# An attention and gated-MLP kernel on one core: the opening written in another order, with fillers on TensorE, the first rest values pooled by GpSimd, and the last weight loaded in halves

## The chip, the cores and the metric

The kernel runs on one core of a Trainium2 chip. The metric is the time of one execution in microseconds on the device. Three runs of the kernel before are shown, with their median, and one further execution was profiled.

The engines are named as the profile names them: PE (TensorE, matrix products), PEld (its weight loads), DVE (VectorE), ACT (ScalarE), POOL (GpSimd) and SP, whose queue issues nearly all transfers.

## The reference

```python
def _attn_ref(q, k, v):                       # q, k, v: 8 x 8 x 576 x 64
    k_p = k.reshape(B, H, S // 8, 8, D).mean(axis=3)
    v_p = v.reshape(B, H, S // 8, 8, D).mean(axis=3)
    scores = np.matmul(q, k_p.transpose(0, 1, 3, 2)) / np.sqrt(D)
    scores = scores - np.max(scores, axis=-1, keepdims=True)
    attn = np.exp(scores)
    attn = attn / (np.sum(attn, axis=-1, keepdims=True) + 1e-09)
    return np.matmul(attn, v_p).astype(np.float32)

def _moe_ref(x, w_in, w_out):                 # 4608 x 512, 512 x 2048, 2048 x 512
    h = x @ w_in
    g = h * np.clip(h + 3.0, 0.0, 6.0) / 6.0
    return (g @ w_out).astype(np.float32)
```

Keys and values are means over 8 positions, so each of the 8 batches has 72 keys. The attention's output, 8 batches of 576 tokens by 512, is the x of the second function. The two weights come as 64-bit floats.

## The kernel before

**Precision.** The large products take fp32r operands, each value split into a high and a low part; a product is three matmuls (high by high, high by low, low by high). x, g and the weights are split this way. Batch 0's scores, transposes and attention products use plain float32.

**Blocks and steps.** The 4608 tokens are cut into blocks of 512, 256 and then ten of 384 (L22). The weights stay on the chip, in 16 slices f of 128 hidden columns. A step (`Step`, L584) is one slice for one block: `h` (12 matmuls into a bank of PSUM), `relu` on ACT, `gate` on DVE, `hi` on ACT, `lo` on DVE, and `out` (three matmuls for each tile of 128 tokens, added up over the slices). `run` (L788) goes through a block's steps; `out` follows two steps behind `h`. Between the matmuls `slot` places the attention of the next block, piece by piece.

**The first block** carries more. Its 512 tokens belong to batch 0 and are two parts, A (tokens 0 to 255) and B (256 to 511). Their attention is done in the opening, L676 to L766. Its steps also prepare the weights, since each slice arrives as 64-bit words. For one slice `Prep` (L480) does `scale` and `low` on ACT, `sign` and `join` on DVE, then `hi` on ACT and `lo` on DVE, each over 1024 columns (w_in's half and w_out's half together). Slice 0 alone is loaded and prepared in two halves of 512 columns. During the block's later steps batch 1's keys and values are loaded and pooled.

**What sets the order.** A planner orders the instructions of each engine by its own timeline, within the dependencies. Inside `in_order()` (L89) the instructions of PE, DVE and ACT keep the order in which they are written: each gets a dependency on the one before it on its engine. POOL and SP are left to the planner there too. The whole opening is written out this way; so are `relu` to `lo` and the weight preparation of the first block's steps (L798), and the pooling of batch 1's keys and values (L144, L252). Each engine takes its instructions one after another, so an instruction that waits holds up all behind it.

**The opening, in order.** `busy(13)` writes 13 products of the identity into a bank that nobody reads, while the first transfers run. Then `prep_k` pools the keys (DVE) and ACT scales them into `kbd`. A has four score tiles (two tiles of tokens, two groups of heads): `product` on PE, `top` on DVE (the negated maximum), `exps` on ACT (four exponents with their sums), `invert` on DVE, `divide` on POOL or DVE. `FirstValues` pools batch 0's values on PE: `heads` adds eight slices by products with the identity, `place_heads` copies them on ACT; `rest` does the same for the 8 keys of each head that don't fit 64 rows, and `place_rest` masks them on DVE into `vrem`. `transposes` turns the attention on PE and copies it out (DVE or ACT). `av` is the attention product, two float32 matmuls for each of four columns of heads, with the second one reading `vrem`; `put_x` splits the result into `xhi` (ACT) and `xlo` (DVE). Slice 0's step for A follows, a[0], with B's scores, transposes and `av` around it. The second half of slice 0, for B, is the first step of `run`; its `h` isn't in written order, so the planner sets its matmuls between others.

**Memory.** The first loads lie in regions ("stage") that later hold weights 7 to 14. The region of slice 15 holds the work tile `u` of the preparation, two halves for even and odd slices. So slice 15 can be loaded only when slice 14 is done with `u`. In `run`, step 13 (k = 15) loads it whole, and prepares it in two parts: `scale` to `join` in the same step, `hi` and `lo` in the next.

## Time and profile before

| | us |
|---|---|
| median of three runs | 963.69 |
| lowest, highest | 961.54, 964.84 |
| the profiled execution | 961.42 |
| its span, first to last instruction | 959.6 |

The mean granted clock of the profiled execution is 0.993 of full speed. Where the busy shares of PE are below nine tenths in the page's 40 slices (24 us each), the slices are the first three and the last:

```profile
PE   8799989999999999999999999999999999999998
PEld 6577768899999999999999999999999998999996
DVE  5788975747424437436433444634633442442221
ACT  4578755645334426435435345434534453532322
POOL 1000340403001103102201010300300110110000
PEclk9899999999999999999999999999999999999999
```

A row is one engine and a digit the tenths of a slice in which it was busy; in the last row a digit is the granted clock in tenths. Times below are microseconds from the first instruction. A line such as "L555" is a line of the kernel before. In rows of grouped instructions stand the count, then busy time and the mean in nanoseconds, then the idle time ahead of them and what ended it.

### The profile page before, as it was taken

The numbers are of one execution on the slowest core, as the hardware profiler recorded it, in microseconds if no ns is written. First come the engines' busy times: TensorE is split into PE (matmuls) and PEld (weight loads), VectorE is DVE, ScalarE is ACT, GpSimd is POOL, SyncE is SP. The second block draws the span as 40 slices with busy tenths as digits, with TensorE's granted clock in tenths as the row PEclk, the third lists the DMA queues.
The fourth block names the chain that finished last, engine by engine and source line by source line (L and its number), as shares of the span: only waits on it lengthen the run. The fifth ranks groups of instructions, "written<-read, shape, count | busy, mean of one in ns | idle before, by whom it ended". The sixth has DMA issues, their size and how long they took to land.

```text
span 959.6 us, 13759 instructions
## 1 busy us (share of the span) xinstructions
PE 936.5 (98%) x4934; PEld 832.6 (87%) x4934; DVE 467.4 (49%) x986; ACT 448.0 (47%) x1388; POOL 130.4 (14%) x247
## 2 busy tenths in 40 slices
PE   8799989999999999999999999999999999999998
PEld 6577768899999999999999999999999998999996
DVE  5788975747424437436433444634633442442221
ACT  4578755645334426435435345434534453532322
POOL 1000340403001103102201010300300110110000
PEclk9899999999999999999999999999999999999999
DMA  9942013313001104004001004102201000100000
GB/s 338 397 158 67 17 45 105 95 36 107 12 26 31 35 1 153 24 1 153 12 1 55 12 24 129 48 1 93 72 1 37 19 23 1 45 1 1 33 1 33
DMA packets 42452, 58.57 MB, mean 61 GB/s; under 512 B 3600, under 2 KB 24080, under 8 KB 42384
## 3 DMA queue, kind: packets, MB, share of 16 engines
q1 hardware_dynamic: 42240, 57.69, 18.0%
q8 instruction: 39, 0.64, 0.3%
q14 instruction: 29, 0.24, 0.1%
q10 hardware_dynamic: 144, 0.00, 0.0%
HBM read 48.24 MB, written 9.44 MB: 60 GB/s over the span
## 4 chain that ended last, share of the span: by engine, by line
PE 82%; DVE 4%; ACT 3%; DMA 1%; issue 1%; SPq 0%; ACTq 0%; POOL 0%; DVEq 0%
PE pso L626 37%; PE psh L597 37%; PE psa L415 3%; PE psa L295 3%; PE psa L368 2%; DVE w L555 1%; ACT e L303 1%; DVE u L516 1%; ACT raw L522 1%; DMA vst<-v_l 1%; DVE vst L253 1%; DVE g L609 1%; ACT u L511 0%; DMA raw<-w_out_l 0%; DVE u L527 0%
## 5 line engine op out<-in xcount | busy, mean ns | idle before, releaser
L597 PE MATMUL psh<-xhi,w 128*128 128x384 f32 (+2 forms) x1544 | 432.3, 340 | 7.5 <-DVE w L555 5.0
L626 PE MATMUL pso<-w,ghi 128*128 128x512 f32 x1152 | 360.6, 402 | 2.1 <-ACT ghi L613 2.1
L597 PEld LDWEIGHTS psh<-xhi,w 128*128 128x128 f32 x1544 | 281.0, 189 | 23.9 <-DVE w L555 7.8
L597 PE MATMUL psh<-xlo,w 128*128 128x384 f32 (+2 forms) x772 | 260.0, 337 | 0.0
L626 PEld LDWEIGHTS pso<-w,ghi 128*128 128x128 f32 x1152 | 207.2, 188 | 33.7 <-ACT ghi L613 2.3
L605 ACT ACTIVATE g<-psh,small 128x384 f32<-128x384 f32 (+2 forms) x193 | 112.5, 583 | 240.3 <-PE psh L597 240.0
L626 PE MATMUL pso<-w,glo 128*128 128x512 f32 x576 | 219.6, 396 | 1.2 <-DVE glo L617 1.2
L609 DVE SCALAR_TENSOR_TENSOR g<-g,psh 128x384 f32<-128x384 f32 (+2 forms) x193 | 106.1, 550 | 225.4 <-ACT g L605 224.5
L597 PEld LDWEIGHTS psh<-xlo,w 128*128 128x128 f32 x772 | 146.0, 189 | 9.9
L613 ACT CAST ghi<-g 128x384 fp32r<-128x384 f32 (+2 forms) x193 | 99.5, 516 | 74.2 <-DVE g L609 71.8
L617 DVE TENSOR_TENSOR glo<-g,ghi 128x384 fp32r<-128x384 f32 (+2 forms) x193 | 108.9, 565 | 51.6 <-ACT ghi L613 49.4
L329 POOL TENSOR_TENSOR a<-e,sm 128x256 f32<-128x256 f32 x72 | 47.7, 663 | 634.6 <-DVE sm L320 407.7
L626 PEld LDWEIGHTS pso<-w,glo 128*128 128x128 f32 x576 | 107.7, 188 | 27.8 <-DVE glo L617 2.8
L303 ACT ACTIVATE e<-psa,mx 128x72 f32<-128x72 f32 x288 | 89.2, 330 | 52.6 <-DVE mx L299 50.3
L299 DVE TENSOR_REDUCE mx<-psa 128x4 f32<-128x288 f32 x80 | 35.2, 453 | 56.0 <-PE psa L295 55.8
L303 ACT ACTIVATION_READ_ACCUMULATOR e<-psa,mx 128x1 f32 x288 | 61.6, 214 | 0.0
L409 DVE TENSOR_TENSOR xlo<-psa,xhi 128x192 fp32r<-128x192 f32 (+3 forms) x68 | 29.6, 438 | 37.8 <-ACT xhi L408 37.7
L253 DVE TENSOR_REDUCE vst<-vst 128x64 f32<-128x512 f32 (+1 forms) x42 | 44.8, 1072 | 6.1 <-DMA vst<-v_l 3.4
L408 ACT CAST xhi<-psa 128x192 fp32r<-128x192 f32 (+3 forms) x68 | 25.9, 384 | 45.2 <-PE psa L415 44.4
L295 PE MATMUL psa<-kbd,qt 128*128 128x144 f32 x280 | 43.4, 286 | 0.4 <-ACT kbd L153 0.4
L295 PEld LDWEIGHTS psa<-kbd,qt 128*128 128x128 f32 x280 | 40.6, 189 | 2.1 <-ACT kbd L153 0.6
L379 DVE TENSOR_TENSOR alo<-psa,ahi 128x256 fp32r<-128x256 f32 (+1 forms) x70 | 27.7, 396 | 24.4 <-ACT arem L378 24.3
(67 smaller groups left out, 620.1 us busy)
## 6 DMA issues: line engine op xcount, KB each, us to landing
qt<-q_l SPq DMA_DIRECT2D x36, 256.0 KB, 3.5
out<-o SPq DMA_DIRECT2D x36, 256.0 KB, 2.1
raw<-w_in_l SPq DMA_DIRECT2D x16, 512.0 KB, 10.1
raw<-w_out_l SPq DMA_DIRECT2D x16, 512.0 KB, 10.1
kst<-k_l SPq DMA_DIRECT2D x28, 288.0 KB, 3.7
vst<-v_l SPq DMA_DIRECT2D x28, 256.0 KB, 3.9
vst<-vr_l SPq DMA_DIRECT2D x42, 64.0 KB, 1.9
stage<-k_l SPq DMA_DIRECT2D x4, 288.0 KB, 3.4
```

Of the source, the lines that this page charges most:

```text
L253: nc.vector.tensor_reduce(out=vs, in_=st[:n, : POOL * D].rearrange("p (o d) -> p d o", o=POOL), axis=AX.X, op=ALU.add)
L295: nc.tensor.matmul(to, qt[:, p, :], kbd[:, p, :], start=True, stop=True)
L299: nc.vector.tensor_reduce(out=self.mx, in_=self.ps, axis=AX.X, op=ALU.max, negate=True)
L303: nc.scalar.activation(self.e[:, h], self.ps[:, h], AF.Exp, bias=self.mx[:, h : h + 1], accum_out=self.sm[:, h : h + 1])
L329: engine.tensor_tensor(out=self.a[:, : 4 * D].rearrange("p (h s) -> p h s", h=4), in0=e[:, :, :D], in1=sm[:, :, None].broadcast_to([P, 4, D]),
L409: nc.vector.tensor_tensor(out=xlo, in0=ps, in1=xhi.bitcast(F32), op=ALU.subtract)
L597: nc.tensor.matmul(self.ps, l[f][:, c, :], r[:, c, :], start=c == 0 and i == 0, stop=c == NCC - 1 and i == 2)
L605: nc.scalar.activation(self.g, self.ps, AF.Relu, bias=half, scale=1.0 / (6.0 * WSCALE))
L609: nc.vector.scalar_tensor_tensor(out=g, in0=g, scalar=1.0, in1=self.ps, op0=ALU.min, op1=ALU.mult)
L613: nc.scalar.copy(self.ghi, self.g)
L617: nc.vector.tensor_tensor(out=self.glo, in0=self.g, in1=self.ghi.bitcast(F32), op=ALU.subtract)
L626: nc.tensor.matmul(pos, l, r[f], start=f == 0 and i == 0, stop=f == NF - 1 and i == 2)
```

## The change

The change has four parts.

1. **The opening in another order.** After A's score products six fillers are written, five more ahead of B's first `av`, and two ahead of its last two. B's first score product moves ahead of A's `av`, the second and third between and behind them, over more banks. Slice 0's preparation starts earlier (its first `scale` and `low`, and the second `scale`, ahead of `place_heads`; `sign` and `join` ahead of A's transposes), and its second half is finished later, between B's softmaxes. B's softmaxes all use `exps`, the form with sums on ACT. All of B's `av` moves ahead of the second half of slice 0, whose `h` is now in written order (in `run`, for steps of part of a block). Slice 1 is fully prepared at the end of the opening, `hi` and `lo` too, and `run` skips what is prepared (the set `prepared`). For B's last two `av` the low part of x is written down behind slice 1's `hi`.
2. **The rest's values on POOL.** `rest` adds the eight slices in three halving steps in place and masks them, all on POOL; `place_rest` and the products on PE are gone.
3. **Batch 1's pooling** of keys and values is no longer in the written order.
4. **The last slice** is loaded in two tiles, one for each half of `u`. Both transfers are written one step earlier (k = 14); the first half needs only slice 13 to be done with `u`, the second slice 14. The first half is prepared wholly in step 13, the second half in steps 13 and 14.

```diff
@@ -141,10 +141,9 @@
         if i == 0:
             ksum[b, g] = pool.tile([P, 2, SP], F32, name="ksum", bufs=1)
         ks = ksum[b, g]
-        with in_order() if b == 1 else nullcontext():
-            nc.vector.tensor_reduce(
-                out=ks[:, i], in_=kraw.pop((b, p)).rearrange("p (s o) -> p s o", o=POOL), axis=AX.X, op=ALU.add
-            )
+        nc.vector.tensor_reduce(
+            out=ks[:, i], in_=kraw.pop((b, p)).rearrange("p (s o) -> p s o", o=POOL), axis=AX.X, op=ALU.add
+        )
         if i == 1:
 
             scale = 1.0 / (POOL * D**0.5)
@@ -227,14 +226,14 @@
                 nc.scalar.mul(self.v32[rows, :, h * D : (h + 1) * D], self.ps[rows], 1.0 / POOL)
 
         def rest(self):
-            self.pr = att_bank()[:REM, : NG * D].rearrange("p (g d) -> p g d", g=NG)
-            self.add(self.pr, vraw[0, NPAIR])
-
-        def place_rest(self):
+
+            raw = vraw[0, NPAIR]
+            for w in (4 * D, 2 * D, D):
+                nc.gpsimd.tensor_tensor(out=raw[:, :, :w], in0=raw[:, :, :w], in1=raw[:, :, w : 2 * w], op=ALU.add)
             for g in range(NG):
-                nc.vector.tensor_tensor(
+                nc.gpsimd.tensor_tensor(
                     out=self.vrem[:, g].rearrange("p (h d) -> p h d", h=4),
-                    in0=self.pr[:, g, None, :].broadcast_to([REM, 4, D]),
+                    in0=raw[:, g, None, :D].broadcast_to([REM, 4, D]),
                     in1=mask[:REM, 2:6, None].broadcast_to([REM, 4, D]),
                     op=ALU.mult,
                 )
@@ -249,10 +248,9 @@
         n, h = (P, 2) if p < NPAIR else (3 * REM, 4)
         st = vraw.pop((b, p))
         vs = st[:n, POOL * D : (POOL + 1) * D]
-        with in_order() if b == 1 else nullcontext():
-            nc.vector.tensor_reduce(
-                out=vs, in_=st[:n, : POOL * D].rearrange("p (o d) -> p d o", o=POOL), axis=AX.X, op=ALU.add
-            )
+        nc.vector.tensor_reduce(
+            out=vs, in_=st[:n, : POOL * D].rearrange("p (o d) -> p d o", o=POOL), axis=AX.X, op=ALU.add
+        )
         m = mask[:n, :2] if p < NPAIR else mask[:n, 2:6]
         raw = st[:n, : h * D]
         nc.gpsimd.tensor_tensor(
@@ -403,17 +401,16 @@
             mms = [(whi[:, p], hi[:, i, :T]), (whi[:, p], lo[:, i, :T]), (wlo[:, p], hi[:, i, :T])]
         return mms + [(wrem[:, g, i * P : (i + 1) * P], rem[:, :T])]
 
-    def put_x(j, T, x0, p, ps):
-        xhi, xlo = (t[:, p, x0 : x0 + T] for t in x_block(j))
-        nc.scalar.copy(xhi, ps)
-        nc.vector.tensor_tensor(out=xlo, in0=ps, in1=xhi.bitcast(F32), op=ALU.subtract)
-
-    def av(j, b, h0, T, x0, p):
+    def av(j, b, h0, T, x0, p, later=None):
+
         ps = att_bank()[:, :T]
         mms = av_sums(b, h0, T, p)
         for n, (l, r) in enumerate(mms):
             nc.tensor.matmul(ps, l, r, start=n == 0, stop=n == len(mms) - 1)
-        put_x(j, T, x0, p, ps)
+        xhi, xlo = (t[:, p, x0 : x0 + T] for t in x_block(j))
+        nc.scalar.copy(xhi, ps)
+        low = lambda: nc.vector.tensor_tensor(out=xlo, in0=ps, in1=xhi.bitcast(F32), op=ALU.subtract)
+        low() if later is None else later.append(low)
 
     def side_steps(b):
 
@@ -463,13 +460,14 @@
 
 
     def groups(f):
-        return [(0, 1), (1, 2)] if f < SPLIT else [(0, 2)]
+        return [(0, 1), (1, 2)] if f < SPLIT or f == NF - 1 else [(0, 2)]
 
     def w_tile(name, f, a, b, shape, dtype):
-        return const.tile([P, b - a] + shape, dtype, name=f"{name}_{f}", tag=f"w_{f}_{a}" if f < SPLIT else f"w_{f}")
+        tag = f"w_{f}" if (a, b) == (0, 2) else f"w_{f}_{a}"
+        return const.tile([P, b - a] + shape, dtype, name=f"{name}_{f}", tag=tag)
 
     def load_w(f):
-        wraw[f] = []
+        wraw.setdefault(f, [])
         for a, b in groups(f):
             raw = w_tile("raw", f, a, b, [DM, 2], U32)
             wraw[f].append((a, b, raw))
@@ -489,15 +487,13 @@
 
 
         def __init__(self, f):
-            self.f, self.raws, self.made = f, wraw.pop(f), {}
-            if f == 0:
-                ubuf.append(const.tile([P, 2, 2 * DM], F32, name="u", tag=f"w_{NF - 1}"))
-            if f == NF - 1:
-                _, _, raw = self.raws[0]
-                self.parts = [(i, i + 1, raw[:, i : i + 1], ring("u")[:, :DM]) for i in range(2)]
-            else:
-                u = ubuf[0][:, f % 2]
-                self.parts = [(a, b, raw, u[:, a * DM : b * DM]) for a, b, raw in self.raws]
+            self.f, self.made = f, {}
+            if f < 2:
+                ubuf.append(const.tile([P, 2 * DM], F32, name="u", tag=f"w_{NF - 1}_{1 - f}"))
+            last = f == NF - 1
+            self.parts = [
+                (a, b, raw, ring("u")[:, :DM] if last else ubuf[f % 2][:, a * DM : b * DM]) for a, b, raw in wraw.pop(f)
+            ]
 
         def words(self, part):
             _, _, raw, u = part
@@ -558,13 +554,17 @@
 
     preps = {}
 
+    prepared = set()
+
     def prep(f, *stages, part=None):
+
         if f not in preps:
             preps[f] = Prep(f)
-        parts = preps[f].parts
         for s in stages:
-            for x in parts if part is None else parts[part : part + 1]:
-                getattr(preps[f], s)(x)
+            for n, x in enumerate(preps[f].parts):
+                if part in (None, n) and (f, s, n) not in prepared:
+                    prepared.add((f, s, n))
+                    getattr(preps[f], s)(x)
 
 
     n_h = [0]
@@ -673,6 +673,7 @@
     values = FirstValues()
     first = Block(0, ["o0", "o1", "o2", "o3"])
     a = [Step(first, f, 0, 2) for f in range(SPLIT)]
+    by_act = nc.scalar.copy
     with in_order():
         busy(13)
         for p in range(NPAIR):
@@ -680,6 +681,7 @@
         x00, x10, x01, x11 = (Scores(*t[:2], g) for g in range(NG) for t in tiles(A))
         for x in (x00, x10, x01, x11):
             x.product()
+        busy(6)
         x00.top()
         x00.exps()
         x10.top()
@@ -702,68 +704,75 @@
         x11.invert()
         x11.divide(nc.vector)
         values.rest()
+        prep(0, "scale", "low", part=0)
+        prep(0, "scale", part=1)
         values.place_heads()
+        prep(0, "sign", "join", part=0)
         T0, T1 = tiles(A)
         transposes(*T0, 0, 0)
         transposes(*T1, 0, 0)
-        values.place_rest()
-        prep(0, "scale", "low", part=0)
-        transposes(*T0, 1, 0, nc.scalar.copy)
-        transposes(*T1, 1, 0, nc.scalar.copy)
-        prep(0, "sign", "join", "hi", "lo", part=0)
+        transposes(*T0, 1, 0, by_act)
+        transposes(*T1, 1, 0, by_act)
+        prep(0, "hi", "lo", part=0)
+        turn = [(t, g) for g in range(NG) for t in tiles(B)]
+        b = [Scores(*t[:2], g) for t, g in turn]
+        att_banks[:] = ["h0", "o0", "o1", "o2", "a0", "a1"]
+        b[0].product()
         av(0, *A, 0)
-        prep(0, "scale", part=1)
+        b[0].top()
+        b[1].product()
         av(0, *A, 1)
-        prep(0, "low", part=1)
+        b[0].exps()
+        b[1].top()
         av(0, *A, 2)
         av(0, *A, 3)
-        prep(0, "sign", "join", "hi", part=1)
-        att_banks[:] = ["a0", "a1", "o2", "o3"]
-        turn = [(t, g) for g in range(NG) for t in tiles(B)]
-        b = [Scores(*t[:2], g) for t, g in turn]
-        b[0].product()
-        b[1].product()
-        a[0].h()
+        att_banks[:] = ["o0", "o2"]
         b[2].product()
-        b[3].product()
-        b[0].top()
-        b[0].exps()
-        prep(0, "lo", part=1)
-        b[1].top()
-        b[1].shift()
-        a[0].relu()
-        a[0].gate()
-        b[1].exp()
-        a[0].hi()
         b[0].invert()
         b[0].divide(nc.gpsimd)
-        a[0].lo()
-        b[1].total()
+        b[1].exps()
+        a[0].h()
+        b[2].top()
+        b[3].product()
         b[1].invert()
         b[1].divide(nc.vector)
-        b[2].top()
+        prep(0, "low", part=1)
+        a[0].relu()
         b[2].exps()
+        a[0].gate()
         b[3].top()
-        b[3].shift()
-        b[3].exp()
+        att_banks[:] = ["a0", "a1", "h0"]
+        transposes(*turn[0][0], turn[0][1], 256)
+        transposes(*turn[1][0], turn[1][1], 256, by_act)
+        prep(0, "sign", "join", part=1)
+        a[0].hi()
+        b[2].invert()
+        b[2].divide(nc.gpsimd)
+        prep(0, "hi", part=1)
+        a[0].lo()
+        b[3].exps()
+        prep(0, "lo", part=1)
+        busy(5)
+        av(0, *B, 0)
+        av(0, *B, 1)
+        prep(1, "scale", "low")
+        b[3].invert()
+        b[3].divide(nc.vector)
         a[0].out()
         att_banks[:] = ["a0", "a1"]
-        transposes(*turn[0][0], turn[0][1], 256)
-        transposes(*turn[1][0], turn[1][1], 256, nc.scalar.copy)
-        b[2].invert()
-        b[2].divide(nc.gpsimd)
-        b[3].total()
-        b[3].invert()
-        b[3].divide(nc.vector)
-        prep(1, "scale", "low", "sign")
-        av(0, *B, 0)
-        av(0, *B, 1)
         transposes(*turn[2][0], turn[2][1], 256)
-        transposes(*turn[3][0], turn[3][1], 256, nc.scalar.copy)
-        prep(1, "join")
-        av(0, *B, 2)
-        av(0, *B, 3)
-        prep(2, "scale", "low", "sign")
+        transposes(*turn[3][0], turn[3][1], 256, by_act)
+        prep(1, "sign", "join")
+        prep(2, "scale")
+        later = []
+        busy(2)
+        av(0, *B, 2, later)
+        av(0, *B, 3, later)
+        prep(1, "hi")
+        for low in later:
+            low()
+        prep(1, "lo")
+        prep(2, "low", "sign")
     for f in range(4, NF - 1):
         load_w(f)
 
@@ -794,24 +803,30 @@
             slot = paced.slot if u >= first_slot else no_slot
             if u < len(steps):
                 x, k = steps[u], preps.get(u)
-                x.h(slot)
+                with in_order() if x.n < x.blk.nt * P else nullcontext():
+                    x.h(slot)
                 with in_order() if x.blk.j == 0 else nullcontext():
                     if k:
                         prep(k - 1, "hi", "lo")
+                    if k == NF - 1:
+                        prep(k, "scale", "low", part=0)
                     x.relu()
                     x.gate()
-                    if k and k < NF - 1:
+                    if k == NF - 1:
+                        prep(k, "sign", "join", part=0)
+                    elif k:
                         prep(k, "join")
                     x.hi()
                     x.lo()
                     if k and k + 1 < NF - 1:
                         prep(k + 1, "scale", "low", "sign")
-                    if k == NF - 1:
-                        load_w(k)
-                    if preps and u == len(steps) - 3:
-                        prep(NF - 1, "scale", "low", "sign", "join")
+                    if k == NF - 2:
+                        load_w(NF - 1)
+                    elif k == NF - 1:
+                        prep(k, "hi", "lo", part=0)
+                        prep(k, "scale", "low", "sign", "join", part=1)
                     elif preps and u == len(steps) - 2:
-                        prep(NF - 1, "hi", "lo")
+                        prep(NF - 1, "hi", "lo", part=1)
             if u == len(steps) - 1:
                 paced.upto(len(attention))
             if u >= lag:
```

## The prediction

> **What bounds the kernel now.** I read the page first, then the waits of PE, then the windows.
>
> ```profile
> span 959.6 us, 13759 instructions
> PE 936.5 (98%) x4934; PEld 832.6 (87%) x4934; DVE 467.4 (49%) x986; ACT 448.0 (47%) x1388; POOL 130.4 (14%) x247
> PE pso L626 <- ACT ghi L613: 2.1, 1, 2.1
> PE psa L415 <- ACT a L373: 2.1, 1, 2.1
> ```
>
> PE is busy for 98% of the span, so only 23 us of idle time exist. Its longest waits in the opening (each row: us in total, times, longest) are 2.1 us for the gated values and 2.1 us for the transposed attention. A second loss is not idle time: the granted clock. In the windows the columns are the stretch, its length, PE, PEld, DVE, ACT and POOL busy, then the clock.
>
> ```profile
> 28.20:31.60 3.40, 2.10 (x10) 1.38 (x11) 3.05 (x11) 1.04 (x3) 0.99 (x2) 1.00 1.03 411
> 31.60:35.00 3.40, 1.29 (x8) 0.68 (x7) 2.78 (x10) 3.01 (x13) 0.81 (x2) 1.00 1.03 411
> 35.00:38.40 3.40, 3.40 (x7) 1.45 (x8) 2.03 (x4) 1.78 (x4) 0.00 (x0) 0.50 1.03 405
> 45.20:48.60 3.40, 1.48 (x8) 0.82 (x7) 2.89 (x4) 3.40 (x11) 0.00 (x0) 1.00 1.09 367
> 48.60:52.00 3.40, 3.06 (x7) 2.51 (x8) 2.44 (x8) 3.40 (x15) 1.21 (x3) 0.51 1.04 410
> 55.40:134.00 78.60, 72.67 (x322) 57.45 (x321) 69.71 (x95) 58.28 (x113) 19.50 (x20) 0.98 0.12 36
> 130.50:133.90 3.40, 2.82 (x7) 2.27 (x8) 2.86 (x4) 1.97 (x3) 3.32 (x2) 0.51 0.01 2
> 134.00:154.00 20.00, 19.54 (x102) 16.22 (x100) 10.90 (x22) 10.38 (x33) 2.51 (x5) 1.00 0.20 66
> ```
>
> A stretch in which PE was busy for 1.29 or 1.48 of 3.4 us is followed by one at half clock; after 2.10 the clock stayed. From 55.4 to 134 PE lacks 5.9 us and DVE is busy for 69.7 of 78.6: here two engines are near their limit. From 134 to 154 only 0.5 us is missing. So three stages can gain: the opening, the first block's middle, and hardly the last weight.
>
> The Trainium skill, "TensorE: Matmul & The Clock Gate" (HAM oscillation), warns of PE gaps above about 3.4 us. By that rule gaps of 2.1 us would not have slowed anything and fillers would be worth nothing; the rows above disagree, and the measurement decides.
>
> **The opening.** I write the new order out as a timetable: each engine takes its instructions in the written order, an instruction starts when its engine and its inputs are ready, I allow 0.06 us from engine to engine, and durations are those of before at full clock.
>
> ```profile
> 2.38 5.70 PE L203 MATMUL idle<-ident 128*128 128x128 f32 x26 [2.38 <-POOL ident masks.py:199]
> 7.92 2.13 PE L295 MATMUL psa<-kbd,stage 128*128 128x144 f32 x16
> 11.67 5.55 PE L218 MATMUL psa<-stage,ident 128*128 128x256 f32 x32 [1.62 <-DMA stage<-v_l]
> 15.29 1.66 PEld L218 LDWEIGHTS psa<-stage,ident 32*32 32x32 f32 x16 [0.33 <-issue]
> 17.15 1.53 PE L368 MATMUL psa<-ident,stage 128*128 128x128 f32 x12
> 18.64 0.67 PE L415 MATMUL psa<-a,v 128*128 128x256 f32 x2
> 23.62 1.25 PE L295 MATMUL psa<-kbd,stage 128*128 128x144 f32 x8
> 26.07 1.14 PE L295 MATMUL psa<-kbd,stage 128*128 128x144 f32 x8
> 45.17 0.28 PE L597 MATMUL psh<-xhi,w 128*128 128x256 f32 x1
> 15.46 0.77 ACT L227 ACTIVATE v<-psa 64x256 f32<-64x256 f32 x2 [3.16 <-PE psa L218]
> 17.74 0.76 DVE L373 COPY a<-psa 128x256 f32<-128x256 f32 x2 [3.05 <-PE psa L368]
> raw<-w_in_l SPq DMA_DIRECT2D x1, 512.0 KB, 5.8
> raw<-w_out_l SPq DMA_DIRECT2D x1, 512.0 KB, 6.3
> ```
>
> PE's terms: a filler is 5.70/13 = 0.44 us. Six of them run from 10.05 (7.92 + 2.13) to 12.6; the values land at 11.67, so they cost 0.9 us there. The sums of heads take 15.29 - 11.67 = 3.6; the small sums of the rest (15.29 to 17.15, 1.9 us) leave PE. Four transposes take 18.64 - 17.15 = 1.5, a score product 2.13/4 = 0.53, four 'av' 23.62 - 18.64 = 5.0. The 'h' of 256 tokens began after two score products at 23.62 + 1.06 = 24.7 and ended at 26.07, 1.4 us; 'out' of two tiles has half its matmuls, each of twice the columns, so I put it at 1.4 too (an estimate). The new order then reads:
>
> 10.05 + 2.6 fillers + 3.6 heads + 1.5 transposes + 2.1 products of B + 5.0 av + 1.4 h + 1.5 transposes of B + 2.2 for five fillers + 5.0 av of B + 1.4 out + 0.9 for two fillers + 1.4 h of the second half = 38.7 us, if PE never waits. Before, that 'h' ended at 45.17 + 0.28 = 45.5.
>
> Does PE wait? ACT's 'scale' and 'low' of weight 0 now stand ahead of place_heads. The halves were issued at 7.22 and 8.10 and land 5.8 and 6.3 us later, at 13.0 and 14.4; three operations of about 0.65 are done by 15.1, and the heads are summed at 16.2. Their cover is ACT's idle 3.16 us; a landing over 1.1 us later would push place_heads back by the excess. 'sign' and 'join' (0.69 each) lie in DVE's idle 3.05 us; without it they would delay the first attention copies by 1.4. What queues behind an input not yet there: the transposes' copies, then av. Followed through all three queues, av of B starts at 29.0 with its last copy ready at 28.4, 'out' at 31.5 with its last input at 30.3, and one wait remains, 0.4 us for the copies of B's last transposes. So 39.1.
>
> From there ACT and DVE set the time, by preparing weights.
>
> ```profile
> L303 ACT ACTIVATE stage<-psa,mx 128x72 f32<-128x72 f32 x16 | 4.9, 322 | 3.8 <-DVE mx L299 3.8
> L522 ACT ACTIVATE raw<-raw 128x1024 f32<-128x1024 f32 x4 | 4.6, 1159 | 0.0
> 52.60 1.23 DVE L516 SCALAR_TENSOR_TENSOR u<-raw,u 128x1024 uint32<-128x1024 uint32 x1 [1.55 <-ACT u L511]
> 53.74 1.22 DVE L555 TENSOR_TENSOR w<-u,w 128x1024 fp32r<-128x1024 f32 x1
> ```
>
> Four exponents take 4.9/4 = 1.2 us, an ACT pass over a weight 1.1, and a DVE pass starts 53.74 - 52.60 = 1.14 after the one before. ACT's queue after A's last x copy (24.1): exponents 25.3, half a 'low', relu and exponents 27.6, copies of B's first transposes 28.4, ghi and half a 'hi' 29.6, exponents 30.8, two x copies of B 31.9, 'scale' and 'low' of weight 1 34.0. DVE's 'sign' and 'join' of it end at 36.4; ACT copies the rest of B's x by 37.9, 'hi' ends at 38.9, DVE's 'lo' at 40.1. Weight 2 on DVE: 'sign' and 'join' 2.3, the half step's gate and glo 0.8, 1.1 of waiting for ACT's 'low' of weight 3, that weight's 'sign' and then 'lo' 2.3: 46.6. Before, weight 2's 'lo' ended at 53.74 + 1.22 = 55.0. **Opening: 46.6 - 55.0 = -8.4 us.** From there both orders have the same work ahead, so the whole rest shifts.
>
> The bounds: PE's idle pieces between 39 and 46.7 come to 3 us, at most 1.55 of them in one stretch of 3.4: a busy 1.85, between the 1.48 that slowed the clock and the 2.10 that did not. A stretch at half clock costs up to 1.7. And if the six fillers buy nothing, their 0.9 is the loss.
>
> **The rest's values on POOL**: per pair three additions and two products on 32 partitions, which the trace does not show. The nearest rows:
>
> ```profile
> 13.84 0.24 POOL L335 TENSOR_TENSOR stage<-stage,sm 128x32 f32<-128x32 f32 x1
> L272 POOL TENSOR_TENSOR vrem<-vst,vrem 32x256 fp32r<-32x256 f32 x2 | 3.1, 1562 | 0.1
> L272 POOL TENSOR_TENSOR vrem<-vst,vrem x14: 727/742/2380, 131.6 to 685.2; 32x256 fp32r<-32x256 f32 x14
> ```
>
> The additions have 512, 256 and 128 elements a partition. By the median 0.74 for 256: 1.5 + 0.74 + 0.4 + 2 x 0.74 = 4.1 us; by the 1.56 of the two in the first block, 8.6. POOL is free at 14.1 (13.84 + 0.24), so they end at 18.2 or 22.7; the first av's second product wants them at 18.8. I take 4.1, since the median is that of 14 and the 1.56 of a crowded DVE: no delay; the other end costs 3.9. Ended ahead of x01's 'divide' instead, they would delay that by about as much as it has to spare.
>
> The Trainium skill, "SBUF — State Buffer" (Who interferes with whom), speaks against this move: a DVE instruction with two SBUF inputs and a POOL instruction that reads SBUF exclude one another. DVE's 'sign' and 'join' stand just there. The two L272 rows bear the rule out in kind; by it the 3.9 would be more likely.
>
> **The first block's middle.** Pooling batch 1's keys and values leaves the written order; the planner places it.
>
> ```profile
> L253 DVE TENSOR_REDUCE vst<-vst 128x64 f32<-128x512 f32 x4 | 4.3, 1065 | 0.0
> L516 DVE SCALAR_TENSOR_TENSOR u<-raw,u 128x1024 uint32<-128x1024 uint32 x11 | 14.1, 1279 | 7.0 <-ACT u L511 6.9
> 126.49 2.92 DVE L253 TENSOR_REDUCE vst<-vst 128x64 f32<-128x512 f32 x3
> 131.08 1.22 PE L597 MATMUL psh<-xhi,w 128*128 128x512 f32 x2 [3.19 <-DVE w L555]
> ```
>
> Three pinned reductions at 126.49 stand ahead of the 'lo' that PE awaits for 3.19 us until 131.08. DVE idles 6.9 us behind 'low' in this stage; reductions that slide in there no longer delay 'lo'. At best PE's 5.9 us and the 1.7 of half clock return, 7.6; but then DVE would be busy for 69.7 of 71. At worst the planner puts each of six value reductions (about 1.07, of which a slot hides little) just ahead of a 'lo': +5, six times some 0.85. I take -2.5, most of the 3.19 stall.
>
> **The last weight.** Its first half's transfer leaves a step earlier; with 0.5 us missing from 134 to 154 I count 0, ends -0.5 and +1 (ACT in line behind the second half's transfer; PE's queue of 'out' covers more than that).
>
> **Sum.** The profiled execution took 961.42 (span 959.6): 961.4 - 8.4 - 2.5 = 950.5. The median of the runs, 963.69, lies 2.3 above it, the mean of all four 1.5; I add that and say 952.
>
> **The rivals.**
> 1. POOL's values come late: for it, DVE's two-input operations beside them; against it, 0.6 us to spare. +1 to +3.9, about 955.
> 2. The freed reductions give part back. For: DVE has little room. Against: the stall that they make now is the longest of the stage. +5 in place of -2.5: about 959.5.
> 3. Slower: the planner puts the value reductions ahead of their transfers, and DVE stands, the weights' preparation behind it.
>
> ```profile
> vst<-v_l SPq DMA_DIRECT2D x4, 256.0 KB, 2.7
> vst<-vr_l SPq DMA_DIRECT2D x6, 64.0 KB, 1.9
> DMA vst<-v_l: 3.4, 9
> ```
>
> Price: four of 2.7 and two of 1.9, 14.6, and the -2.5 is lost: 952 + 17.1 = 969. It decides from 11 us on, three quarters of those transfers. Against it: DVE's unpinned value reductions of later batches waited for such transfers 3.4 us in nine cases altogether.
> 4. The change does nothing, its fillers only taking the place of waits while ACT's queue is as late as before: 963 to 964. The 39.1 for 45.5 speaks against it.
>
> **How the numbers follow.** Forecast 0.64 (947 to 955), rival 1 0.13, rival 2 0.13, rival 3 0.07, rival 4 0.03. A measurement of this kernel tells about 0.3%, 2.9 us, from no change; rival 2 lies at that bound, half of it on either side. Faster 0.64 + 0.13 + 0.06 = 0.83, same 0.07 + 0.03 = 0.10, slower 0.07. The range runs from 946.5, the middle's best end with a little kept back, to 959, which takes in the forecast, rival 1 and some of rival 2.
>
> **What would show it.** Right: weight 2's 'lo' ends near 46.6; no PE wait above 1 us between 12 and 38, and no half clock there; POOL's last operation on the rest ends by 18.8; no PE wait above 2 us in the rest of the block. Wrong: an opening that gains under 5 us breaks the timetable; PE waiting for vrem is rival 1; DVE waiting for vst is rival 3.

## The result and the profile after

The kernel after takes 947.01 us (median of four runs, 946.30 to 947.97), the kernel before 962.65 in the same comparison (961.54 to 964.84, four runs): a ratio of 0.9835, interval 0.9812 to 0.9859. The profiled execution fell from 961.42 to 947.71, its span from 959.6 to 945.9.

The page of the kernel after, and its waits of PE in the first 200 us (us in total, times, longest):

```profile
span 945.9 us, 13775 instructions
PE 931.2 (98%) x4944; PEld 831.6 (88%) x4944; DVE 465.5 (49%) x980; ACT 449.3 (47%) x1402; POOL 130.6 (14%) x252
PEclk9998999999999999999999999999999999999999
```

```profile
PE psa L366 <- POOL vlo L265: 3.1, 1, 3.1
...
PE psa L409 <- DVE a L371: 1.3, 1, 1.3
```

The two waits of 2.1 are gone. In the clock row the low slice is the fourth, where it was the second. A new wait of 3.1 has come. Its windows of the same stretches (columns as before):

```profile
31.60:35.00 3.40, 3.38 (x18) 2.29 (x17) 2.42 (x9) 3.40 (x11) 0.31 (x1) 1.00 1.03 408
...
45.20:48.60 3.40, 2.80 (x17) 1.86 (x15) 2.92 (x5) 2.44 (x6) 0.44 (x2) 1.00 1.10 371
55.40:134.00 78.60, 75.46 (x345) 62.15 (x344) 71.51 (x104) 61.33 (x132) 17.32 (x24) 0.96 0.17 52
73.60:77.03 3.43, 1.03 (x7) 0.72 (x5) 3.43 (x6) 0.68 (x5) 3.43 (x4) 1.00 0.22 59
77.03:80.45 3.42, 2.68 (x8) 2.31 (x9) 3.13 (x7) 2.60 (x10) 3.17 (x6) 0.50 0.41 107
80.45:83.86 3.41, 3.41 (x9) 2.64 (x9) 3.41 (x5) 3.24 (x7) 2.03 (x3) 0.50 0.14 33
134.00:154.00 20.00, 20.00 (x117) 17.47 (x116) 8.94 (x20) 10.12 (x32) 0.69 (x2) 1.00 0.38 124
```

In the opening TensorE is now nearly full and at full clock. At 73.6 it stands, and the clock is halved for the next 6.8 us.

To see where the time went, I note when TensorE reaches the same amount of work in both kernels. Work is the sum of the usual start-to-start spacing of the products, without fillers and without the rest's small sums (a reckoning from the rows of both traces, us):

```
work done    before    after   difference
    8         19.86    20.16      +0.3     A's scores and heads
   56         80.63    72.60      -8.0     opening
   60         85.16    81.86      -3.3     the new stop and its half clock
  100        133.81   123.08     -10.7     before's stop at 127.9, half clock
  104        137.85   127.04     -10.8     end of the middle
  152        189.81   175.66     -14.2     last weight, rest of the block
  500        540.08   525.98     -14.1     nothing more
```

So 8.0 come from the opening, 2.8 from the middle and 3.3 from the last weight. After the first block nothing changes.

### The profile page after: what moved, and what is told of

Its sections match the earlier page's. It is cut to its first block, busy times and chain, and to the rows that moved or that the text cites. A ratio compares the mean times of both kernels' runs of the same rounds, so it can differ in the third digit from the quotient of the medians.

```text
span 945.9 us, 13775 instructions
## 1 busy us (share of the span) xinstructions
PE 931.2 (98%) x4944; PEld 831.6 (88%) x4944; DVE 465.5 (49%) x980; ACT 449.3 (47%) x1402; POOL 130.6 (14%) x252
## 4 chain that ended last, share of the span: by engine, by line
PE 93%; DVE 3%; ACT 2%; issue 1%; DMA 1%; POOL 0%; SPq 0%; ACTq 0%; POOLq 0%
PE pso L626 41%; PE psh L597 41%; PE psa L409 4%; PE psa L293 4%; PE psa L366 2%; DMA stage<-q_l 1%; DVE u L512 0%; DVE u L523 0%; DVE w L551 0%; DVE mx L297 0%; ACT u L507 0%; DVE vst L251 0%; DVE ksum L144 0%; ACT w L546 0%; ACT e L301 0%
## 5 line engine op out<-in xcount | busy, mean ns | idle before, releaser
L327 POOL TENSOR_TENSOR a<-e,sm 128x256 f32<-128x256 f32 x72 | 47.9, 665 | 616.8 <-DVE sm L318 401.1
L317 DVE TENSOR_SCALAR sm<-sm 128x4 f32<-128x4 f32 x80 | 15.2, 190 | 50.7 <-ACT e L301 50.4
## 6 DMA issues: line engine op xcount, KB each, us to landing
raw<-w_in_l SPq DMA_DIRECT2D x16, 512.0 KB, 10.1
raw<-w_out_l SPq DMA_DIRECT2D x16, 512.0 KB, 10.1
```

The lines of the kernel that those rows point to most:

```text
L327: engine.tensor_tensor(out=self.a[:, : 4 * D].rearrange("p (h s) -> p h s", h=4), in0=e[:, :, :D], in1=sm[:, :, None].broadcast_to([P, 4, D]),
```

## The experiments

Each is compared with the kernel before on the same chip (its median there was 964.2 to 964.7); behind a ratio stands its 95% interval. The first eight take a part back or make one part alone; the last four ask what the new stop is.

**No fillers.** `busy(6)`, `busy(5)` and `busy(2)` are removed from the kernel after.

> The changed kernel (947.0) with its thirteen fillers taken out; nothing else differs. Theory: the fillers keep the granted clock up. Without them PE's waits in the opening leave stretches with too little work, one or two of them of 3.4 us at half clock, and the kernel takes 2 to 5 us longer (949 to 952), with PEclk below 1.00 somewhere between 12 and 45 us. Rival: the fillers only occupy waits, and the first six stand on the path by about 0.5 us, so that without them the time is 946.0 to 947.5 and the clock stays at 1.00 in the opening.

Measured: 947.22 (946.82 to 951.63), ratio 0.9825 (0.9791 to 0.9860). The median is the rival's, not the 2 to 5 us more of the theory: the fillers make no difference there, and in the profiled execution the clock stays whole in the opening without them. The two waits of 2.1 are gone here too, so it isn't the fillers that took them away. One run of four is 4 us longer, so I came back to this below.

**The rest's values back on PE.**

```diff
-    for w in (4 * D, 2 * D, D):
-        nc.gpsimd.tensor_tensor(...)
+    self.add(self.pr, vraw[0, NPAIR])     # on PE, masked by DVE behind A's first transposes
```

> The changed kernel with the rest's values summed by PE and masked by DVE again, in a PSUM bank of its own. Theory: POOL's operations hold up DVE's two-input operations, so that A's divide takes 1.45 us instead of 0.42 and the first av starts 1.4 us later than in my timetable; putting the sums back costs PE 1.9 us in front of the transposes and gives that 1.4 back: within 1 us of 947, with A's divides on DVE near 0.45 us. Rival: POOL's pooling is free and PE's 1.9 us is simply added: 948.5 to 949.5.

Measured: 948.85 (946.87 to 949.25), ratio 0.9825 (0.9791 to 0.9859). That lies in the rival's range and outside the theory's, but its interval takes in the ratio of the kernel after, so the time gives no verdict. The traces tell what is exchanged. First A's part of the opening in the kernel after (the timeline: start, length), then in this one:

```profile
12.66 1.26 POOL L232 TENSOR_TENSOR stage<-stage 32x512 f32<-32x512 f32 x1 [9.83 <-DVE sm L317]
12.77 1.45 DVE L327 TENSOR_TENSOR stage<-stage,sm 128x256 f32<-128x256 f32 x1
15.87 1.10 DVE L327 TENSOR_TENSOR stage<-stage,sm 128x256 f32<-128x256 f32 x1
17.04 2.18 POOL L234 TENSOR_TENSOR vrem<-stage,small 32x256 f32<-32x256 f32 x2
17.76 0.99 DVE L523 SCALAR_TENSOR_TENSOR u<-raw,u 128x512 uint32<-128x512 uint32 x1
19.56 0.67 PE L409 MATMUL psa<-a,v 128*128 128x256 f32 x2 [1.32 <-DVE a L371]
```

```profile
12.19 0.43 DVE L327 TENSOR_TENSOR stage<-stage,sm 128x256 f32<-128x256 f32 x1
14.04 0.42 DVE L327 TENSOR_TENSOR stage<-stage,sm 128x256 f32<-128x256 f32 x1
15.20 0.69 DVE L523 SCALAR_TENSOR_TENSOR u<-raw,u 128x512 uint32<-128x512 uint32 x1
18.88 0.60 PE L409 MATMUL psa<-a,v 128*128 128x256 f32 x2
```

Beside POOL's operations DVE's divides take 1.45 and 1.10 instead of 0.43 and 0.42, the `join` 0.99 instead of 0.69: 2.0 us more in DVE's queue, of which TensorE waits 1.3. On PE the sums cost 1.9, nothing waits, and A's first `av` starts 0.7 us earlier. By work 56 the version on PE is 0.7 us behind, but in between its trace has a stretch of half clock from 24.53 (shown in the last section), across which it falls back by 1.5. Nor is the wait of 1.3 a fixed price: in the second profiled execution of the kernel after (below) TensorE waits 0.3 there, and this `av` starts at 18.87. So the slower operations of DVE are shown; that the move to POOL gains anything isn't.

**Batch 1's pooling in written order again** (opening and halves are left).

```diff
+    with in_order() if b == 1 else nullcontext():     # around both tensor_reduce
```

> The changed kernel with batch 1's pooling of keys and values back in the written order. Theory: freeing it gave the 2.9 us that the middle of the first block gained (PE stalls before, about 9 us with the clock, against about 6 after): 949 to 951, with a PE wait above 2 us on a weight's low part near 118 us and none near 75. Rival: the new stall at 74.6 us (3.1 us and half clock behind it, some 6 us) is worse than what pinning costs now that the opening is earlier: 943 to 946.

Measured: 952.91 (950.21 to 954.57), ratio 0.9871 (0.9838 to 0.9904). Freeing is worth 4.5 to 5.9 in this kernel by the medians (against 948.40 and 947.01, the two measurements of the kernel after), more than expected; by the ratios it is 3.5 (0.9871 to 0.9835), and their intervals still touch. Its wait of 3.2 for a weight's low part near 120 is the old stop.

**The last weight whole and a step later** (opening and freed pooling are left).

```diff
-    return [(0, 1), (1, 2)] if f < SPLIT or f == NF - 1 else [(0, 2)]
+    return [(0, 1), (1, 2)] if f < SPLIT else [(0, 2)]
-    if k == NF - 2: load_w(NF - 1)
+    if k == NF - 1: load_w(k)
```

> The changed kernel with the last weight loaded whole a step later and prepared as before. Theory from the two traces: after the preparation of weight 14 the change gained a further 3.3 us of PE time, and the last weight is the cause: 949.5 to 951, with DVE idle about 4 us behind 'low' of the last weight. Rival, my prediction's term: it is worth nothing, and the 3.3 us come from where the planner puts the next blocks' attention: 946.5 to 947.5.

Measured: 954.64 (953.35 to 964.63), ratio 0.9913 (0.9888 to 0.9937): further from the kernel after than even the theory had it. Between work 104 and 152 its trace loses 7.1 us against the kernel after. (Its profile has a stretch of half clock in the opening besides, 4.4 us, shown further down; the median doesn't hang on it.) How the wait runs through the engines, in its waits and its timeline:

```profile
PE psh L598 <- DVE g L610: 4.3, 3, 2.2
PE pso L627 <- DVE glo L618: 1.6, 2, 1.2
```

```profile
135.56 0.66 ACT L519 ACTIVATE raw<-raw 128x512 f32<-128x512 f32 x1 [2.16 <-DMA raw<-w_in_l]
138.71 1.29 DVE L513 SCALAR_TENSOR_TENSOR u<-raw,u 128x512 uint32<-128x512 uint32 x2 [4.58 <-ACT u L508]
141.86 0.39 PE L598 MATMUL psh<-xhi,w 128*128 128x256 f32 x1 [2.21 <-DVE g L610]
```

ACT waits for the transfers (a second time, 1.25, for `w_out`'s at 137.46), DVE's `sign` waits for ACT, DVE's gate stands behind `sign`, and TensorE waits for the gate. For the kernel after the view of waits shows none of TensorE from 122 to 176.

**Only V's pooling in written order,** K's free.

> The kernel after, with the V pooling of batch 1 kept in its written order on VectorE and the K pooling free. Theory: the freed V reductions come in a bunch (six from 68.7 to 81.8), their masks go to POOL ahead of the attention's divides, and that makes TensorE's 3.1 us stop at 74.6 and the half clock from 77.0; with V in its written order both go (about -6.4), and some of the pinned kernel's 3.2 us stop near 120 with its half clock comes back: 941 to 947, and no TensorE wait over 1 us from 70 to 85. Rival: it is the K reductions (56.1 and 62.0) that brought the bunch; then the stop at 75 stays and V only adds its stop near 120: 950 to 953.

Measured: 949.02 (947.51 to 949.41), ratio 0.9848 (0.9813 to 0.9883). The stop at 75 and its half clock are gone, so V's bunch makes them. But the old stop of 3.2 and a half clock from 123.0 come back (another half clock stands at 47.9, in the opening), and the time lies above the expected 941 to 947.

**Each part of the change alone,** on the kernel before: the halves; the freed pooling; the opening with the rest on POOL.

> The kernel before, with the last weight alone changed: its two halves loaded a step earlier and prepared a step apart. Theory: the last weight loses TensorE 3.8 us between the products of 108 and 152 us of work in the trace of before and 0.7 in that of after, so the halves alone bring about 3 us wherever they are put: 959 to 962 where the kernel before has 962.7, and VectorE's wait of 3.95 behind ScalarE's part of the last weight is gone. Rival: in the kernel before the block's other work stands over that wait, and the gain needs the new opening: within 1 us of the kernel before.

> The kernel before, with the pooling of batch 1 freed and nothing else. Theory: with the last weight loaded whole, freeing the pooling only brings the block sooner to the place where VectorE waits for that weight (as 955.3 with the opening alone and 954.6 with opening and freed pooling have it): no more than 2 us below the kernel before, 962 to 965. Rival: freed pooling is worth what it is worth in the kernel after, 4.5 to 5.9, whatever the last weight does: 957.5 to 960.

> The kernel after with K and V pooling of batch 1 back in written order and the last weight whole and a step later: the new opening with the rest on POOL is all that is left of the change. Theory: the parts add up, by what TensorE lost in the traces (4.5 for the pooling, 7.1 for the last weight, each taken back alone): 947.0 + 11.6 = 958.6, 956.5 to 960.5. Rival: the two share one loss, since one late weight hides the other; then it comes out at the kernel before less the opening's 8: 953 to 955.5.

The first two came out as the theory had them, the third as its rival had it (953 to 955.5): the parts don't add up. All versions of the three parts together:

```
opening  pooling free  halves     us       ratio (interval)
   -          -          -       964.5     1
   -          -         yes      960.77    0.9968 (0.9946 to 0.9990)
   -         yes         -       962.92    0.9990 (0.9975 to 1.0004)
  yes         -          -       955.29    0.9916 (0.9889 to 0.9943)
  yes         -         yes      952.91    0.9871 (0.9838 to 0.9904)
  yes        yes         -       954.64    0.9913 (0.9888 to 0.9937)
  yes        yes        yes      947.01    0.9835 (0.9812 to 0.9859)
```

The rows were measured on several chips, and the last one beside a kernel before of 962.65, so the ratios compare better than the times. The halves are worth 3.7 us alone and 6.2 to 7.6 where pooling is freed; there the two intervals don't touch. Freed pooling is worth nothing that can be told, neither alone nor on the new opening, as long as the last weight is loaded whole; with the halves it is worth the 3.5 to 5.9 of above. For the new opening the rows show a reason: the attention's products ("psa") alone, from 128 to 160 us, in the kernel before, with the last weight whole, with the opening alone, and with freed pooling alone.

```profile
128.00:160.00 32.00, 3.68 (x25) 3.55 (x26) 2.83 (x8) 4.31 (x22) 0.95 0.13 42
```

```profile
128.00:160.00 32.00, 0.00 (x0) 0.00 (x0) 0.00 (x0) 0.00 (x0) 1.00 0.20 65
```

```profile
128.00:160.00 32.00, 4.81 (x32) 4.42 (x33) 2.82 (x8) 4.31 (x22) 1.00 0.29 94
```

```profile
128.00:160.00 32.00, 1.79 (x11) 1.62 (x11) 0.70 (x2) 0.97 (x6) 1.00 0.09 33
```

With pooling in written order the next block's attention is late, so that 25 to 32 of its products lie beside the last weight; from about 130 to 190 us TensorE waits 1.9 us for values of the gate in the kernel before (2.8 with the opening alone). On the new opening with pooling freed they are done by 128, none is left, and TensorE waits 5.9 (4.3 + 1.6 above). That the products fill the wait is read from these counts; no run moved them alone. And on the old opening the reason doesn't reach: with freed pooling alone 11 products are left and TensorE waits 2.7, only 0.8 more than in the kernel before. In that execution, by the reckoning of work, the opening, which the edit doesn't reorder, is 2.6 us behind (13.7 us at half clock from 35.5); in the middle the freed pooling first loses 6.1 and then gains 8.4, and the last weight costs 0.5 more. So there it is mostly waits of its own that eat the gain, as far as one execution tells.

**POOL's masks behind the divides,** added to the kernel after.

```diff
+    if engine is nc.gpsimd: divided[:] = [the divide's last instruction]
+    if b == 1: behind(V's mask, divided[0])
```

> The kernel after, with one rule more for POOL: a mask of batch 1's V pooling stands behind the last divide of the attention that is written before it. Theory: TensorE's stop at 74.6 is the divide behind three masks and their lows; with the divide first the stop (3.1) goes, and with it the half clock behind it (another 3.3): 940.5 to 944.5, no TensorE wait over 1 us from 70 to 85. Rival: the masks are only late in another place (V's staging tiles come free later, and the products of batch 1 wait for V's low parts near 105): 946 to 950.

Measured: 947.58 (946.13 to 950.67), ratio 0.9840 (0.9800 to 0.9881); span 944.3. The time is the rival's. The stop in the kernel after, by its timeline:

```profile
72.78 1.05 DVE L251 TENSOR_REDUCE vst<-vst 128x64 f32<-128x512 f32 x1
72.86 0.40 POOL L256 TENSOR_TENSOR vst<-vst,small 128x128 f32<-128x128 f32 x1 [0.80 <-DVE sm L318]
73.22 0.62 POOL L327 TENSOR_TENSOR a<-e,sm 128x256 f32<-128x256 f32 x1
73.75 1.21 DVE L512 SCALAR_TENSOR_TENSOR u<-raw,u 128x1024 uint32<-128x1024 uint32 x1
73.79 2.53 POOL L333 TENSOR_TENSOR a<-e,sm 128x96 f32<-128x96 f32 x1
74.89 1.22 DVE L551 TENSOR_TENSOR w<-u,w 128x1024 fp32r<-128x1024 f32 x1
76.35 0.32 ACT L301 ACTIVATE e<-psa,mx 128x72 f32<-128x72 f32 x1 [2.76 <-DVE sm L317]
77.46 0.21 ACT L301 ACTIVATION_READ_ACCUMULATOR e<-psa,mx 128x1 f32 x1
77.77 0.87 PE L366 MATMUL psa<-ident,a 128*128 128x128 f32 x3 [3.14 <-POOL vlo L265]
79.85 0.34 POOL L333 TENSOR_TENSOR a<-e,sm 128x96 f32<-128x96 f32 x1
```

The divide's second half takes 0.34 by itself; here it takes 2.53, and ends just behind two operations of DVE that lie back to back (73.75 to 76.11). The Trainium skill, "SBUF — State Buffer" (Who interferes with whom), says that a DVE instruction with two SBUF inputs excludes a POOL instruction that reads SBUF, and a reduction doesn't; the rows agree, since POOL's 0.62 lay beside the reduction unhurt. One mask (0.40) ahead of the divide, as I read it, pushed it out of the reduction's shadow into that pair. TensorE starts 1.45 us behind the divide's end, and its transposes read nothing of the `vlo` that their row names. As I read it, the program has two buffers of exponents and two banks for the attention here: the divide frees a buffer at 76.3, ACT's next exponents run from 76.35 to 77.67, and then a bank is free for the transposes. The same link stands by name in the kernel with the masks behind:

```profile
72.72 0.32 ACT L305 ACTIVATE e<-psa,mx 128x72 f32<-128x72 f32 x1 [1.27 <-POOL a L337]
```

There that divide is done at 72.7, TensorE's longest wait on POOL from 70 to 85 is 0.9, and the clock stays whole to the kernel's end. But the bunch of V reductions still fills DVE, and the waits for weights are new:

```profile
PE psh L603 <- DVE w L557: 2.8, 3, 1.6
```

So the stop went as the theory had it, but the wait moved from POOL to DVE: by the reckoning of work the 4.3 us gained at the stop have shrunk to 0.4 by about work 76, where TensorE has waited for weights. Of the 1.6 us by which the profiled span is shorter, 1.2 are there already at A's first `av` (18.32 for 19.56), in the opening, where the edit changes nothing. The median gains nothing.

**The kernel after again.**

> The kernel after once more, as the measure for e12 on the same chip and for how far its runs spread: 946.3 to 948 by every theory. By the theory that a half-clock stretch depends on how a wait lies to a clock of its own, some runs have the second stretch and some have none: runs from 943.5 to 951, in steps of about 3.4.

Measured: 948.40 (945.47 to 951.62), ratio 0.9839 (0.9812 to 0.9866); the median lies just above what was expected. Three runs lie at 945.5 to 945.7 with a mean clock of 0.997, three at 951.1 to 951.6 with 0.995 and 0.992 twice. There are two levels, but 5.8 us apart and not one stretch of 3.4. Only one of the lower runs was profiled, so what the upper ones have besides wasn't seen.

**V's reductions, one in each step,** in the kernel after.

```diff
+    glos.append(the instruction of glo)                  # in Step.lo
+    if b == 1: behind(V's reduction, glos[5 + p])        # in prep_v
```

> The kernel after, with each V reduction of batch 1 held behind the low part of one step's gated values, a step later for each (the first behind the sixth such part): not in a bunch as in after, and not late as in written order. Theory: the stop of 3.1 at 74.6 came from the bunch (on POOL in after, on VectorE in the kernel with the masks behind the divides), so with one reduction in a step both go: no TensorE wait over 1 us and no half clock from 60 to 125, 940 to 943.5, that is 3.5 to 6.5 below after in the same call. Rival: VectorE has no room for a reduction in any of these steps, so the wait only moves to the later weights' low parts: within 1.5 of after.

Measured: 945.25 (944.87 to 947.03), ratio 0.9808 (0.9788 to 0.9829). No half clock from 60 to 125; in place of the stop of 3.1 stand three waits, the longest 1.13:

```profile
PE psh L601 <- DVE w L555: 2.1, 3, 1.1
```

The kernel is 3.2 below the kernel after by the medians of one call, just short of the expected 3.5 to 6.5, and above the expected 940 to 943.5; the theory missed that DVE still has no room for a whole reduction. The lower level of the kernel after is the same 945.5. The median of the kernel after lies between its two levels, and the intervals of the two ratios overlap, so that it beats the kernel after isn't shown. It beats the kernel before.

**The same without the fillers,** since this kernel spreads less.

> The kernel e12_v_by_step without the thirteen products of the opening that nobody reads (six, five and two); the first thirteen, which the kernel before has too, stay. Theory: the new written order has taken away the waits that those products would bridge, so they bring nothing: 944.5 to 947 as with them (945.25), no half clock before 60. Rival: they keep the clock full in waits that still stand (1.3 at 18 us): in the runs without them a stretch of half clock of 3.4 or 6.8 us falls into the opening, 1.7 or 3.4 us more in about half of the runs, a median of 946.5 to 949 with runs up to 950.

Measured: 945.83 (943.00 to 947.26, six runs), ratio 0.9820 (0.9790 to 0.9851). Time as the theory had it, but not the clock. Its windows:

```profile
9.14:12.55 3.41, 0.99 (x9) 0.78 (x7) 3.19 (x11) 3.05 (x18) 0.00 (x0) 1.00 1.06 329
12.55:15.96 3.41, 3.15 (x8) 2.55 (x9) 3.27 (x10) 1.66 (x3) 2.66 (x4) 0.50 1.08 358
```

Without the six fillers the stretch behind A's scores is empty and the sums of heads run at half clock; that costs 2.1 us at work 4 against the kernel with them. At work 8 only 0.2 of it is left. What sets the time there I take to be A's softmax and divides on DVE, which don't depend on TensorE's clock; that is argued, not shown. So here the fillers do what they are for, at a place where it isn't needed; the kernel after without fillers, above, kept its clock there in the one execution that was profiled.

## Why the prediction was right or wrong

The forecast was 952.0, in a range from 946.5 to 959.0; 947.01 lies in it, near its lower end, and the direction is right. That it lies there is partly luck: the lower end stood for the best end of the middle, and what brought the time down was the last weight, which the sum had at nothing, and a median below the profiled execution instead of above it.

1. **Opening, -8.4:** right, -8.0 by work 56, and 9.2 by the medians of the runs with the opening alone (964.51 to 955.29). Two errors inside it went against each other: fillers priced too long (2) and A's copies late (3). Of the forecast's events the `h` of the second half ended at 39.8 (39.1 said) and slice 1's `lo` at 40.3 (40.1). Slice 2's `lo` ended at 48.4, not 46.6: the timetable had left out block 1's attention in DVE's queue, with the copies of its transposes and a wait of 1.39 ahead of them:

```profile
45.68 0.29 DVE L371 COPY a<-psa 128x128 f32<-128x128 f32 x1 [1.39 <-PE psa L366]
47.22 1.22 DVE L551 TENSOR_TENSOR w<-u,w 128x1024 fp32r<-128x1024 f32 x1
```

2. **Fillers, 0.44 each, 0.9 on the path:** the size was off. The six take 1.50 us, 0.25 each (from 10.43, in twelve records, two for each), and all thirteen 3.4 where the timetable has 5.7. The thirteen at the kernel's start were no measure for them: these took 5.70 us in the trace of before and 4.57 in that of after. That a wait without fillers would halve the clock came true in one of the two executions profiled without them; that this would cost time didn't.

3. **The rest on POOL, 4.1 us, no delay:** POOL took 4.7 (1.26 + 1.25 + 2.18) and ended at 19.2, not 18.2. TensorE didn't wait for `vrem`; rival 1 came through DVE instead, whose divides and `join` grew by 2.0, and TensorE waited 1.3 (0.3 in the second execution), where the prediction had no wait above 1 us. It was under the bound of 3.9. The 1.9 us that left PE didn't pay for it in this execution: A's first `av` starts at 19.56, against 18.88 with the sums on PE. The sum took little loss because, as far as the rows tell, the fillers were shorter than priced.

4. **Freed pooling, -2.5:** the net is right, -2.8, but as the difference of two larger terms: from work 56 to 104 TensorE lost 9.2 us in the kernel before (57.2 us for 48 of work) and loses 6.4 in the kernel after, 5.3 of them at the new stop and its half clock (work 56 to 60). That is rival 2's mechanism beside the forecast's. "No PE wait above 2 us in the rest of the block" was wrong: 3.14 at 74.6.

5. **Last weight, 0:** this is the step that failed. I read it from 134 to 154, where 0.5 us were missing. The next row of the kernel before, which the prediction didn't look at, has another 1.5:

```profile
154.00:190.00 36.00, 34.48 (x220) 30.21 (x221) 25.77 (x58) 21.36 (x81) 10.28 (x20) 1.00 0.40 126
```

The halves alone are worth 3.7 by the runs, so the term was mis-sized even on the kernel before. And "PE's queue of 'out' covers more than that" isn't, by the counts, what held there: 25 products of the late attention lay beside the wait. The forecast's own step 4 takes them away on the new opening, and then the wait is 5.9. In the traces the term is -3.3, some 1.8 of it at the block's end and 1.5 in the next block's first steps (work 136 to 148); what ties the latter to the weight I didn't trace. Without the halves the kernel after stands at 954.64, 10.1 below the kernel before, near the forecast's 10.9 for the other parts. The parts were added up as if each kept its cover.

6. **+1.5 from the profiled execution to the median:** off by 2.2. The profiled execution after lies 0.7 above the median of its runs, not 1.5 below. The other 2.8 of the 5.0 between forecast and result stand in the profiled execution itself (947.71 for 950.5): step 5's 3.3, less about 0.4 that the opening lacked.

## What to carry to other kernels

A stall that is covered by other late work is priced with its cover gone: when two parts of a change pull the same work forward, neither can be costed from the trace of before alone, and one run with each part left out shows what only both together bring. Work that is set free is placed in a bunch as soon as its data is there; a lower bound for each piece, one in a step, took the longest wait from 3.1 to 1.1 us here, without a gain in time that is shown. And where GpSimd stands on the path, look at what VectorE runs beside it before counting its operation at its usual length.

## What the runs showed of the hardware

The granted clock changes on a raster of 3.41 us that doesn't move with the kernel: in the trace of before stretches of half clock begin at 35.02, 48.67 and 130.59, 4 and 24 raster steps apart, and the raster lies elsewhere in each execution (the half clock of the kernel after begins at 77.03, 1.0 us off the raster of before). A wait of the same length can be followed by half clock or not. In the kernel after a wait of 1.32 at 18.24 is split by the raster (busy 2.40 and 2.80 of 3.41) and the clock stays. In the kernel with the last weight whole nearly the same wait falls into one step:

```profile
17.44:20.85 3.41, 2.09 (x11) 1.24 (x10) 1.69 (x4) 1.90 (x8) 1.53 (x2) 1.00 1.04 414
20.85:24.26 3.41, 3.41 (x10) 1.88 (x8) 1.61 (x4) 0.86 (x5) 0.00 (x0) 0.50 1.04 413
```

A busy 2.09 was followed by 10.2 us at half clock here. But the busy share of a step doesn't decide. With the rest's values on PE, half clock follows two steps in which the profile counts TensorE as busy throughout (the second of them is the first row here); with freed pooling alone, a step with only 1.65 (the last row) is followed by one at full clock:

```profile
21.12:24.53 3.41, 3.41 (x13) 1.73 (x13) 1.53 (x4) 2.00 (x11) 0.00 (x0) 1.00 1.03 411
24.53:27.95 3.42, 3.42 (x17) 3.42 (x17) 2.04 (x8) 2.01 (x10) 0.81 (x2) 0.50 1.03 407
```

```profile
25.26:28.67 3.41, 1.65 (x14) 1.43 (x13) 2.94 (x8) 2.74 (x12) 0.00 (x0) 1.00 1.02 407
```

So the prediction's reading, that 1.48 slows the clock and 2.10 doesn't, is no rule. What decides, and why a halving lasts 3.4, 6.8, 10.2 or (freed pooling alone, from 35.50) 13.7 us, no run tells. The prediction put up to 1.7 us on one stretch of 3.4; this wait was followed by three and cost 4.4 by the reckoning of work.
